# Chunk 0's channel tiles added into one, the softmax expansions kept in spent rows of x, and a new written order

## The chip, the cores and the metric

The kernel runs on one core of a Trainium2 chip. Its five engines work side by side, each through its own list of instructions in order: TensorE (PE: matrix products; its weight loads are listed apart as PEld), VectorE (DVE: elementwise work), ScalarE (ACT: activations and casts), GpSimd (POOL, which here mostly issues DMAs) and SyncE (SP, which only issues DMAs). An engine stops where an instruction has to wait for a semaphore of another engine or of a DMA, and all that is queued behind it stops too. The metric is the device time of one execution in microseconds, the median of several runs.

## The reference

The input x has 2048 rows of 640 bf16 numbers. It is normalised by row; one branch is local attention, the other a two-layer network, and both are added to x.

```python
xn = _layernorm(x, axis=-1)
return x + _A_ref(xn, A_wqkv, A_wo) + _B_ref(xn, B_w1, B_b1, B_w2, B_b2)
```

Attention has 32 heads of 20 channels. Each position looks at 8 positions: itself and those 2, 4, ... 14 rows before; positions before the first are masked.

```python
logits = jnp.einsum("bhsd,bhswd->bhsw", q, kg) * scale
attn = _softmax(logits, axis=-1)
o = jnp.einsum("bhsw,bhswd->bhsd", attn, vg)
```

The network is gelu(xn @ w1 + b1) @ w2 + b2 with 1536 hidden units.

## The kernel before

The 2048 rows are cut into four chunks (n = 0 to 3) of 512, a chunk into four blocks (j, or bl) of 128 rows. Channels lie on the partitions in five tiles of 128, in an order that puts four channels of each of the 32 heads into each tile. The work is cut into 659 small pieces; a string, ORDER (lines 42 to 74), lists their names, and the pieces are issued in exactly that order. Each engine so gets its part of ORDER as its own list. The names, with n the chunk:

- *Norm.* su, ng, sq: sums and squares of a block on ACT (chunks 2 and 3); st: statistics on DVE (chunks 0 and 1); rs: square root on ACT (loads an activation table); rc: reciprocal on DVE; xn: the normalised block on ACT for n > 0 (L266, pool lnp); tc: its transposition, a DMA from SP (L295).
- *Projections.* pj{n}{which}{tile} on PE (L339; which = 0, 1, 2 for q, k, v), five matmuls of 512 columns into a PSUM buffer of pool psA, which has six; pc casts the buffer to SBUF on ACT (L403) and so frees it. hj and hc are the same for halves of chunk 0 (L383, L398). pad copies the 14 columns before a chunk.
- *Logits.* qk{n}{j}{h} on DVE (L436): products of q with four shifted windows of k, all five channel tiles, into half[j, h]. pa{n}{j}{k} on DVE (L471) adds channel tiles: k = 0 adds tiles 2 and 3 onto 0 and 1 (four times 512 columns), k = 1 adds tile 1 onto 0, k = 2 tile 4 onto 0. lg{n} on PE (L479) sums the remaining tiles over channels with the 0/1 matrix head_of, one accumulation step for each tile that is left. KEPT[n] says how many pa steps are made: 2 means k = 0 and 1, and tiles 0 and 4 are left; 1 means all three, and only tile 0 is left.
- *Softmax.* cl casts the logits (ACT, L492), mask (chunk 0 alone), m and mx maximum and its subtraction (DVE, L502 to L508), ex the exponential (ACT, L519, loads a table), ss, ri, at: sum, reciprocal, product (DVE).
- *Values.* xd{n}{j} is a DMA from SP (L554) that spreads a block's weights over each head's channels. Its target, ax_view (L544), is a buffer of its own (pool axp) for chunks 0 and 2, and rows 0 to 6 of x_sb, the loaded x, for chunks 1 and 3. av{n}{j}{h} on DVE (L563) multiplies v's windows by it, again into half. aa adds the two halves: for chunks 0 to 2 as an accumulating DMA issued by POOL (L573), for chunk 3 on DVE (L575). ab and ot (L582, L586) add the rest on DVE; ot writes oT.
- *Network and output.* f1{n}_{ft} on PE (L595), into psA; ge on ACT (L611), which frees that buffer and writes hT (pool hp, 18 buffers; chunk 3 uses spent projection weights). o{n}{bl}{pc} on PE (L631, L633): pc = 0 to 3 multiply hT by w2, pc = 4 multiplies oT by wo. oc casts the sum into osb (ACT, L638), od adds it to the output in DRAM (a DMA from POOL, L644).
- *Output's start.* xp{n} writes rows of x to the output (SP, L304): xp0 rows 0 to 3 of the 16 row blocks, xp1 rows 4 to 7, xp2 rows 8 to 14. xb{n} adds the bias b2 there (POOL, L308). xl adds b2 to the last block on DVE (L311), which oclo and ochi add to the last output.

On DVE the chunks run in pairs: logits of 0, logits of 1, values of 0, values of 1, then the same for 2 and 3, because both use half. The loops are only in the names; what stands when is ORDER's.

Of the kernel before, what the change touches and what calls it, by code (L numbers as in the profile page):

```python
# [23 lines left out]
BPC = CH // P  # L24
# [21 lines left out]
st13a st13 hj112 hc112 st10 st12 rs1 qk010 rc1 qk000 qk011 hj110 f10_0 ge0_0 hj212 xn13 qk001 xn10 tc13 xn11 hc212  # L46
pa010 hj011 hj010 hc010 f10_11 f10_2 hc110 hc011 qk031 qk021 ge0_11 f10_10 qk020 pa000 su23 f10_6 xn12 ge0_10 qk030
pa020 su21 tc10 tc11 su22 hj200 hc200 f10_3 ge0_3 pa030 pa011 f10_9 tc12 xp0 su20 ng2 sq21 ge0_9 pa021 pj101 pc101
ge0_2 sq23 pj111 pj102 pj114 pc114 xp2 pc102 pj110 pc110 pj104 pa001 ge0_6 pa031 lg0 pc111 cl0 ldo xb3 xb2 pc104 mask
m0 mx0 ex0 pj112 pj103 pc103 pj113 pc113 ss0 ri0 pad11 pj100 pc100 pc112 qk121 qk120 hj211 sq20 hc211 qk101 ld2 pj124  # L50
qk100 sq22 pc124 f10_4 rs2 f11_6 pj121 rc2 ge0_4 pa120 qk110 f11_2 f10_1 ge0_1 pa121 qk111 xn21 pj123 pc123 ge1_6
pa122 pa100 pa110 xn23 f10_7 ge0_7 f11_8 tc23 f11_0 o000 xn20 tc20 tc21 ge1_2 f10_5 ge1_0 xb0 xn22 tc22 qk131 at0 xd00
ge1_8 f11_3 ge1_3 pa111 qk130 su32 pa101 pc121 f10_8 ge0_8 pad02 hj210 f11_5 pa130 pj120 pc120 pj200 pc200 pa112 pj211
pc211 pj210 pj212 pa131 pa102 pc210 hc210 pad12 pa132 lg1 av000 cl1 pj202 ge0_5 pj214 pc202 pj204 av001 aa00 m1 xd02
av021 pad21 av020 xd01 av011 av010 pj220 pj203 su33 ge1_5 su31 su30 ng3 sq33 xd03 av031 o001 pc212 pc203 o002 pc214
sq30 ab00 ot00 aa02 aa01 sq32 sq31 pj213 pc213 xp1 pj221 pj224 rs3 av030 ab02 pj122 pc122 pad22 rc3 ot02 o003 o004
oc00 od00 pj201 mx1 ex1 ss1 ri1 at1 xn31 pc220 xn30 f11_9 o020 o021 o022 o023 xd10 ab01 ot01 pc204 o024 oc02 pc201
aa03 tc30 ab03 f11_4 pc224 o030 o031 o032 pj223 o033 ot03 o034 xn33 av100 f12_3 av101 aa10 xn32 pc223 xd12 av120 xd13
f12_0 f11_11 av130 oc03 pc221 o010 o011 ge2_3 f12_11 o012 ge2_11 ge1_4 ge1_9 xd11 av110 av111 aa11 o013 o014 av121
pj222 pc222 av131 aa13 tc31 tc33 tc32 pj302 pj322 pj300 pc322 pj314 pc314 pj312 ab10 f11_1 ge1_11 ge1_1 f11_7 pj303  # L60
qk201 ot10 qk200 pa200 pc312 ge2_0 pj301 pc301 ab11 pa201 f11_10 pc302 ge1_10 qk211 ot11 od02 qk210 ab13 qk231 ot13
pj324 pc324 pj304 pc304 pa210 qk230 aa12 qk221 ab12 ge1_7 pj311 pa211 oc01 ot12 pa230 od01 f13_2 qk220 pc311 f12_8
pa212 od03 ge3_2 pa220 pc300 o130 pa231 pj313 pa221 o131 o132 o133 o134 oc13 pj310 f13_0 pc303 pc310 ge2_8 xb1 o120
pa202 pa232 pa222 lg2 o121 o122 pad31 pc313 qk300 f13_6 qk311 cl2 m2 qk310 f13_10 qk331 mx2 ge3_6 f13_8 qk330 ge3_0
f13_3 ge3_3 pa310 o123 qk301 o124 ex2 ss2 oc12 od12 f12_7 qk320 ri2 pa311 at2 xd23 pa330 pa300 qk321 f12_4 o110 o111
o112 pa301 o113 ge3_10 f12_10 pa320 pa312 o114 oc11 ge2_10 f12_6 f13_7 ge3_7 ge3_8 ge2_7 o100 o101 pa321 f12_2 xd21
od13 pa331 pa302 pa322 f12_5 o102 o103 ge2_6 ge2_5 o104 pa332 lg3 od11 oc10 od10 pj323 av210 pc323 av211 f12_9 cl3 m3
f13_1 xd22 xd20 ge3_1 pj321 av230 f12_1 ge2_1 aa21 av231 f13_5 ge3_5 av201 av200 aa23 f13_9 mx3 ge2_2 ge2_4 aa20 ab21
f13_4 ge2_9 ot21 ex3 ss3 ri3 ge3_4 f13_11 ge3_11 av220 ab23 o210 o211 at3 xd30 o212 o213 o214 ot23 oc21 od21 av221
aa22 pj320 o330 ab20 pc321 ot20 ge3_9 pad32 pc320 av300 o310 av301 o200 o201 o202 o203 o204 oc20 od20 o311 o230 o231  # L70
xd31 av310 o232 xd32 o233 o234 oc23 o312 o220 o221 o222 av311 aa31 ab22 ot22 o223 o224 od23 oc22 od22 av321 o313 av320
aa32 ab32 ot32 o320 o321 o322 o323 o324 oc32 od32 ab31 ot31 o314 oc31 od31 o300 xd33 o301 o302 o303 aa30 av331 ab30
ot30 o304 oc30 od30 av330 aa33 ab33 ot33 o331 o332 o333 o334 ohi xl oclo ochi ochd
""".split()


# [1 line left out]
def kernel(  # L78
# [101 lines left out]
    mask = consts.tile([H, W, MW], BF16, name="mask")  # L180
# [292 lines left out]
    def do_lg(n):  # L473
        tiles["L", n] = [psA.tile([P, W // 2, P], F32, tag="acc", name=f"L{h}") for h in range(2)]
        ts = {KT: range(KT), 3: (0, 1, 4), 2: (0, 4), 1: (0,)}[KEPT[n]]
        for h in range(2):
# [65 lines left out]
        )  # L542

    def ax_view(n):  # L544
        if n % 2 == 0:
            return get(("ax", n), lambda: axp.tile([P, BPC, W, P], BF16, tag="ax", name="ax"))[:]
        return (
            x_sb[:, 0 : 2 * BPC, :]
            .rearrange("p b d -> p (b d)")[:, 0 : BPC * W * P]
            .rearrange("p (j w c) -> p j w c", j=BPC, w=W)  # L550
        )

    def do_xd(n, j):
        nc.sync.dma_start(  # L554
            ax_view(n)[:, j, :, :],
            tiles["attn", n][j * H : (j + 1) * H, :, :].unsqueeze(1).to_broadcast([H, NQ, W, P]),
        )


    def do_av(n, j, h):  # L560
        cs = slice(j * P, (j + 1) * P)
        ws = slice(W // 2 * h, W // 2 * (h + 1))
        nc.vector.tensor_tensor(  # L563
            out=half[:, j, h],
            in0=window(qkv_tile(n, 2), h, cs),
            in1=ax_view(n)[:, j, ws, :].unsqueeze(2).to_broadcast([P, W // 2, KT, P]),
            op=ALU.mult,
        )
# [140 lines left out]
    for n in range(NCH):  # L709
# [87 lines left out]
```

## Time and profile before

| | |
|---|---|
| median of 3 runs | 205.94 us (205.85 to 206.23) |
| the profiled execution | 205.63 us |
| its span, first to last instruction | 203.9 us |
| granted TensorE clock | 0.999 of full speed |
| moved by DMA | 31.77 MB |

The span is what the profile's times count from; some 1.7 us of the execution lie outside it. A row of a group reads: line, engine, operation, output and input, shape and count, then busy us and mean ns of one, then the idle time of the engine before it. A row of the timeline reads: start, time to the end of the last of its instructions, engine, line, operation, count, and in brackets the idle time before it and who ended it. Matmuls overlap, so in the chain of waits a run of them is counted by the time by which it advances.

### The profile page before, as it was taken

The page shows a single profiled execution, that of the slowest core. Times are in us where ns is not written, and L with a number is a line of the kernel's source. Part 1 is how long each engine was busy: PE and PEld are TensorE (multiplying, and loading weights), DVE is VectorE, ACT ScalarE, POOL GpSimd, SP SyncE. Part 2 cuts the span into 40 slices and gives each one's busy share as a digit, 9 for nine tenths or more (in the row PEclk, how much of TensorE's full clock was granted, in tenths as well). Part 3 has the DMA queues.
Part 4 walks back from the last instruction along what each step waited for, and adds up shares of the span by engine and source line. Part 5 has one row for each costly group of instructions (what it writes and reads, how often), then busy time and mean ns, then how long its engine had stood idle before and what let it go on. Part 6 is the DMA issues. An engine that isn't in the chain of part 4 may idle for free.

```text
span 203.9 us, 3209 instructions
## 1 busy us (share of the span) xinstructions
PE 199.0 (98%) x1239; PEld 111.7 (55%) x1261; DVE 181.5 (89%) x226; ACT 127.1 (62%) x246; POOL 34.6 (17%) x49
## 2 busy tenths in 40 slices
PE   8999999999999999999999999999999999999994
PEld 3998565564464555554555554445544455555552
DVE  2699999499998997879999998999999999799991
ACT  5589999999967998856335825473625793111210
POOL 2000000440000243002350060003104224111120
PEclk9999999999999999999999999999999999999999
DMA  6999469899358399999999076005552997972154
GB/s 212 392 395 380 109 217 327 300 259 200 84 112 269 74 172 166 162 146 189 186 178 180 0 88 109 0 0 69 107 130 34 174 190 120 206 110 30 27 66 64
DMA packets 27335, 31.77 MB, mean 156 GB/s; under 512 B 9272, under 2 KB 22072, under 8 KB 27320
## 3 DMA queue, kind: packets, MB, share of 16 engines
q0 software_dynamic: 7408, 12.78, 39.2%
q1 hardware_dynamic: 19600, 18.58, 31.7%
q8 instruction: 10, 0.16, 0.3%
q10 hardware_dynamic: 312, 0.20, 0.3%
q14 instruction: 5, 0.04, 0.1%
HBM read 10.00 MB, written 7.54 MB: 86 GB/s over the span
## 4 chain that ended last, share of the span: by engine, by line
PE 98%; issue 1%; DVE 0%
PE lo L631 28%; PE hps L595 25%; PE pps L339 24%; PE hi L633 8%; PE gps L383 7%; PE idle L449 2%; PE gps L352 1%; PE L L479 1%; PE tp L283 0%; DVE xnT L288 0%; DVE osb L661 0%; PE tb L459 0%
## 5 line engine op out<-in xcount | busy, mean ns | idle before, releaser
L595 PE MATMUL hps<-xnT,w_sb 128*128 128x512 bf16 x234 | 55.2, 379 | 0.3
L436 DVE TENSOR_TENSOR half<-qT,kT 128x2560 bf16<-128x2560 bf16 x32 | 46.6, 1483 | 1.1 <-PE L L479 1.0
L631 PE MATMUL lo<-w_sb,hT 128*128 128x512 bf16 x137 | 40.1, 379 | 0.0
L595 PEld LDWEIGHTS <-w_sb 128*128 128x128 bf16 x240 | 23.1, 98 | 26.2
L471 DVE TENSOR_TENSOR half<-half 128x1024 bf16<-128x1024 bf16 (+1 forms) x44 | 36.5, 878 | 0.0
L633 PE MATMUL hi<-w_sb,hT 128*128 128x128 bf16 x144 | 31.5, 219 | 0.4
L638 ACT CAST osb<-lo 128x512 bf16<-128x512 f32 x15 | 8.8, 583 | 37.1 <-PE hi L633 18.3
L611 ACT ACTIVATE hT<-hps,b1T 128x512 bf16<-128x512 f32 x36 | 24.0, 692 | 6.5 <-PE hps L595 5.6
L644 POOL DMA_DIRECT2D out_dram<-osb x15 | 13.7, 958 | 72.3 <-ACT osb L639 72.3
L563 DVE TENSOR_TENSOR half<-vT,x_sb 128x2560 bf16<-128x2560 bf16 x16 | 23.0, 1486 | 2.8 <-DMA x_sb<-e 2.6
L573 POOL DMA_DIRECT2D half<-half x12 | 15.6, 1302 | 54.9 <-DVE half L563 54.9
L563 DVE TENSOR_TENSOR half<-vT,ax 128x2560 bf16<-128x2560 bf16 x16 | 23.0, 1482 | 1.2 <-PE L L479 1.2
L631 PEld LDWEIGHTS <-hT 128*128 128x128 bf16 x144 | 14.1, 98 | 17.2 <-issue 0.4
L631 PE MATMUL lo<-wo,oT 128*128 128x512 bf16 x75 | 22.3, 379 | 0.1
L339 PE MATMUL pps<-xnT,wq_sb 128*128 128x512 bf16 x74 | 18.5, 379 | 0.1
L339 PE MATMUL pps<-xnT,wv_sb 128*128 128x512 bf16 x73 | 18.2, 379 | 0.1
L339 PE MATMUL pps<-xnT,wk_sb 128*128 128x512 bf16 x74 | 18.0, 379 | 0.1
L633 PE MATMUL hi<-wo,oT 128*128 128x128 bf16 x80 | 16.9, 219 | 0.2
L176 ACT ACT_TABLE_LOAD x12 | 15.4, 1283 | 0.9 <-PEq L781 0.7
L633 PEld LDWEIGHTS <-hT 128*128 128x128 bf16 x144 | 14.1, 98 | 1.9
L582 DVE TENSOR_TENSOR half<-half 128x1280 bf16<-128x1280 bf16 x16 | 13.1, 820 | 0.4 <-DMA half<-half 0.3
L403 ACT CAST vT<-pps 128x512 bf16<-128x512 f32 x15 | 8.8, 586 | 6.9 <-PE pps L339 6.9
(91 smaller groups left out, 263.4 us busy)
## 6 DMA issues: line engine op xcount, KB each, us to landing
half<-half POOLq DMA_DIRECT2D x12, 640.0 KB, 6.8
w_sb<-in_B_w_dram SPq DMA_DIRECT2D x4, 960.0 KB, 11.8
out_dram<-osb POOLq DMA_DIRECT2D x15, 160.0 KB, 3.7
ax<-e SPq DMA_DIRECT2D x8, 256.0 KB, 4.8
x_sb<-e SPq DMA_DIRECT2D x8, 256.0 KB, 4.9
out_dram<-b2bc POOLq DMA_DIRECT2D x3, 640.0 KB, 9.6
x_sb<-in_A_x_dram SPq DMA_DIRECT2D x1, 1280.0 KB, 13.9
out_dram<-x_sb SPq DMA_DIRECT2D x2, 640.0 KB, 4.7
```

Source lines behind the costliest of these rows:

```text
L176: nc.scalar.activation(warm[:], nc.const_aps.tensor(0.0, [P, 1], F32), func)
L339: nc.tensor.matmul(ps[:], lhsT=wqkv_p[which][:, ti, to, :], rhs=xnT[:, ti, :], start=(ti == 0), stop=(ti == KT - 1),)
L383: nc.tensor.matmul(ps[:, to - a, :], lhsT=wqkv_p[which][:, ti, to, :], rhs=tiles["xnT", 0][:, ti, pair * 2 * P : (pair + 1) * 2 * P], star ...
L436: nc.vector.tensor_tensor(out=half[:, j, h], in0=q[:, :, at].unsqueeze(1).to_broadcast([P, W // 2, KT, P]), in1=window(k, h, at), op=ALU.mult,
L471: nc.vector.tensor_tensor(out=kept, in0=kept, in1=gone, op=ALU.add)
L563: nc.vector.tensor_tensor(out=half[:, j, h], in0=window(qkv_tile(n, 2), h, cs), in1=ax_view(n)[:, j, ws, :].unsqueeze(2).to_broadcast([P, ...
L573: nc.gpsimd.dma_start(a, b, accum_op=ALU.add, max_dma_last_dim=CUT)
L595: nc.tensor.matmul(ps[:], lhsT=w1_sb[:, ti, ft * P : (ft + 1) * P], rhs=tiles["xnT", n][:, ti, :], start=(ti == 0), stop=(ti == KT - 1),)
L611: nc.scalar.activation(hT, tiles["hps", n, ft][:], ACT.Gelu_apprx_tanh, bias=b1T[:, ft : ft + 1], scale=1.0)
L631: nc.tensor.matmul(lo[:], lhsT=lhs, rhs=rhs[:, 0:CH], start=first, stop=last)
L633: nc.tensor.matmul(hi[:, 0 : D - CH], lhsT=lhs, rhs=rhs[:, CH:D], start=first, stop=last)
L644: nc.gpsimd.dma_start(rows, tiles["osb", n, bl][:], accum_op=ALU.add)
```

## The change

KEPT[0] goes from 2 to 1, so that four pieces are new, pa002, pa012, pa022 and pa032, and lg0 has one accumulation step instead of two. Chunks 0 and 2 lose their own expansion buffer and use rows 0 to 6 of x_sb; chunks 1 and 3 use rows 8 to 14. The pools of xn, hT and osb have 4, 24 and 3 buffers instead of 3, 18 and 2. ORDER is new behind the first seventy-odd pieces. Line numbers of the new file are lower by 1 from its line 115 on and by 2 behind ax_view.

```diff
-KEPT = (2, 1, 1, 1)
+KEPT = (1, 1, 1, 1)
...
-    lnp = ctx.enter_context(tc.tile_pool(name="lnp", bufs=3))
+    lnp = ctx.enter_context(tc.tile_pool(name="lnp", bufs=4))
...
-    axp = ctx.enter_context(tc.tile_pool(name="axp", bufs=1))
...
-    hp = ctx.enter_context(tc.tile_pool(name="hp", bufs=18))
-    outp = ctx.enter_context(tc.tile_pool(name="outp", bufs=2))
+    hp = ctx.enter_context(tc.tile_pool(name="hp", bufs=24))
+    outp = ctx.enter_context(tc.tile_pool(name="outp", bufs=3))
...
     def ax_view(n):
-        if n % 2 == 0:
-            return get(("ax", n), lambda: axp.tile([P, BPC, W, P], BF16, tag="ax", name="ax"))[:]
+        first = n % 2 * 2 * BPC
         return (
-            x_sb[:, 0 : 2 * BPC, :]
+            x_sb[:, first : first + 2 * BPC, :]
```

ORDER of before, from where the two part to lg1's surroundings:

```
st13a st13 hj112 hc112 st10 st12 rs1 qk010 rc1 qk000 qk011 hj110 f10_0 ge0_0 hj212 xn13 qk001 xn10 tc13 xn11 hc212
pa010 hj011 hj010 hc010 f10_11 f10_2 hc110 hc011 qk031 qk021 ge0_11 f10_10 qk020 pa000 su23 f10_6 xn12 ge0_10 qk030
pa020 su21 tc10 tc11 su22 hj200 hc200 f10_3 ge0_3 pa030 pa011 f10_9 tc12 xp0 su20 ng2 sq21 ge0_9 pa021 pj101 pc101
ge0_2 sq23 pj111 pj102 pj114 pc114 xp2 pc102 pj110 pc110 pj104 pa001 ge0_6 pa031 lg0 pc111 cl0 ldo xb3 xb2 pc104 mask
m0 mx0 ex0 pj112 pj103 pc103 pj113 pc113 ss0 ri0 pad11 pj100 pc100 pc112 qk121 qk120 hj211 sq20 hc211 qk101 ld2 pj124
...
pc211 pj210 pj212 pa131 pa102 pc210 hc210 pad12 pa132 lg1 av000 cl1 pj202 ge0_5 pj214 pc202 pj204 av001 aa00 m1 xd02
```

ORDER of after, from where the two part to behind chunk 1's products with v, and its last stretch:

```
st13a pad02 st13 hj110 hc110 st10 st12 rs1 f10_1 ge0_1 qk001 rc1 qk010 xn11 tc11 qk011 xn10 tc10 qk000 pa010 pa000
f10_2 hj112 xn13 hc112 pa011 xn12 tc12 hj011 hc011 f10_0 ge0_0 hj010 hc010 qk021 hj211 su23 qk030 f10_11 f10_9 ge0_9
hc211 f10_8 ge0_8 qk031 pa012 tc13 qk020 xp0 ldo xb0 pad11 f10_6 pa030 pa020 ge0_2 su22 pj111 ge0_6 pc111 pj103 su20
pj114 su21 ng2 sq23 pa001 ge0_11 pj113 pc113 pa031 pa021 pa002 pj110 f11_11 sq22 pc103 f11_1 xp2 ge1_1 ge1_11 pc110
pa022 f11_5 ge1_5 f10_7 ge0_7 pa032 lg0 cl0 mask pc114 m0 pj104 mx0 ex0 ss0 pj100 pc100 pj112 pc104 pj101 pc101 pj102
pc112 pc102 pj124 f10_4 ri0 qk131 qk110 qk101 f11_0 sq20 sq21 rs2 rc2 ge1_0 xn20 qk121 ld2 o000 qk130 qk111 f11_4
ge1_4 pj123 f10_10 ge0_10 f11_6 ge1_6 xn22 tc20 ge0_4 hj210 xn23 hc210 at0 f11_10 hj212 f10_3 hj200 xn21 hc212 pad12
tc22 qk100 tc23 f10_5 hc200 ge0_5 ge0_3 pa110 pa130 pa100 pa111 pj120 pc120 su32 qk120 pj121 pc121 pa112 tc21 pj200
f12_7 pa120 pj211 pa131 pc124 ge2_7 xd00 xp1 su33 pc211 pa101 pc200 pj213 pa121 pa102 pc123 pj204 pc204 su30 su31
pa132 o001 pa122 lg1 xd03 f12_2 ng3 av000 av001 cl1 xd02 f12_8 ge2_8 ge1_10 ge2_2 aa00 pj122 f12_5 pc213 av020 av021
aa02 pc122 sq32 ge2_5 av030 av031 aa03 pj223 sq30 pj203 m1 mx1 pj202 pc202 ab00 ot00 xd01 av010 pc203 pj210 ex1 pad21
sq31 sq33 rs3 av011 aa01 o002 o003 f11_3 pj214 pc210 pc214 o004 oc00 rc3 xn30 pj220 ss1 ri1 at1 pc220 xn33 xl xd11
pj224 pc224 xd10 pj212 tc33 xd12 ab03 ot03 f11_2 ab02 ot02 ab01 ot01 av111 av101 xn31 xn32 av110 aa11 av120 f12_6 o020
o021 o022 o023 pc212 o024 oc02 f11_8 av121 pad22 o030 tc32 o031 xd13 av100 pc223 o032 o033 o034 oc03 f12_11 ge2_11
o010 o011 o012 aa12 av131 ge1_2 pj201 pc201 ge1_8 tc30 tc31 o013 o014 f13_10 av130 aa13 pj311 pj313 pc311 pc313 ab11
...
o224 o331 av320 av321 aa32 ab32 ot32 o313 oc22 od22 od20 o320 o321 o322 o323 o324 oc32 od32 ot31 o314 o300 o301 o302 o303
av301 oc31 od31 av331 aa30 ab30 ot30 o304 aa33 oc30 od30 ab33 ot33 o332 o333 o334 oclo ohi ochi ochd
```

More of the change, by code (lines that the diff above doesn't have):

```diff
@@ L45 @@
 hc100 xn03 tp03 tc03 pk hj202 rc02 xn02 tp02 tc02 gc4 hj201 hc201 hj111 st11a st10a hc111 st12a hj012 hc012 st11 hc202
[L46 to L73, printed above, removed]
+st13a pad02 st13 hj110 hc110 st10 st12 rs1 f10_1 ge0_1 qk001 rc1 qk010 xn11 tc11 qk011 xn10 tc10 qk000 pa010 pa000
@@ new lines @@
+sq31 sq33 rs3 av011 aa01 o002 o003 f11_3 pj214 pc210 pc214 o004 oc00 rc3 xn30 pj220 ss1 ri1 at1 pc220 xn33 xl xd11
+pj224 pc224 xd10 pj212 tc33 xd12 ab03 ot03 f11_2 ab02 ot02 ab01 ot01 av111 av101 xn31 xn32 av110 aa11 av120 f12_6 o020
+o021 o022 o023 pc212 o024 oc02 f11_8 av121 pad22 o030 tc32 o031 xd13 av100 pc223 o032 o033 o034 oc03 f12_11 ge2_11
+o010 o011 o012 aa12 av131 ge1_2 pj201 pc201 ge1_8 tc30 tc31 o013 o014 f13_10 av130 aa13 pj311 pj313 pc311 pc313 ab11
+pj310 qk211 pj302 pc302 ot11 qk210 qk221 pa210 ab12 f12_4 pa211 ge2_4 qk231 pj303 ge1_3 ab13 ot12 pc303 aa10 ot13 od02
@@ new lines @@
+f12_3 pc310 f11_9 pj324 pc324 f12_0 ge2_0 qk220 qk201 pj312 ab10 od00 ge1_9 pc312 pj300 pc300 pa220 ot10 qk230 qk200
+pa212 pj314 pc314 pa230 xb2 oc01 pj304 pc304 od01 pj301 pc301 pa221 pa200 f13_9 ge3_9 f12_9 pa231 f11_7 ge3_10 pa201
+o130 o131 ge1_7 o132 o133 pa222 pa202 xb3 pad31 pa232 lg2 qk310 qk301 qk311 cl2 m2 qk331 f12_1 o134 oc13 qk300 mx2
+qk320 pj322 pc322 pj321 pj221 pc321 ge2_9 pj222 pc222 ge2_6 xb1 qk321 qk330 ge2_1 o120 od13 pa300 pa330 ex2 ss2 o121
+o122 o123 pa301 ri2 pa302 f13_4 ge3_4 at2 xd21 o124 oc12 od12 f13_8 ge3_8 xd22 f13_7 ge3_7 pc221 pad32 o110 o111 xd20
@@ new lines @@
+o112 o113 o114 oc11 f13_0 pa310 xd23 pa320 o100 od11 o101 o102 ge3_0 o103 o104 oc10 od10 pa311 pa321 pa312 pa322 pa331
+pa332 lg3 av210 f13_2 av211 ge3_2 f13_6 ge3_6 av201 f13_5 ge3_5 cl3 ge2_3 av200 od03 av231 f13_3 ge3_3 m3 mx3 f13_11
+ge3_11 f13_1 pj320 pc320 f12_10 ge2_10 ex3 o210 o211 o212 o213 av230 aa21 ab21 ot21 o214 oc21 pj323 ss3 ri3 at3 aa20
+ab20 o200 o201 ot20 o202 o203 o204 av220 xd33 ge3_1 o330 av221 aa23 ab23 ot23 aa22 pc323 av330 o310 xd30 av300 oc20
+o230 o231 o232 o233 o234 oc23 od23 xd31 av311 o311 o312 av310 aa31 ab31 od21 xd32 o220 o221 o222 o223 ab22 ot22 o224
@@ L74 @@
+o331 av320 av321 aa32 ab32 ot32 o313 oc22 od22 od20 o320 o321 o322 o323 o324 oc32 od32 ot31 o314 o300 o301 o302 o303
+av301 oc31 od31 av331 aa30 ab30 ot30 o304 aa33 oc30 od30 ab33 ot33 o332 o333 o334 oclo ohi ochi ochd
 """.split()
```

## The prediction

> **What bounds the kernel now.** The page comes first: the engines' busy time and the chain that ended last (span 203.9 us).
>
> ```profile
> PE 199.0 (98%) x1239; PEld 111.7 (55%) x1261; DVE 181.5 (89%) x226; ACT 127.1 (62%) x246; POOL 34.6 (17%) x49
> ...
> PE 98%; issue 1%; DVE 0%
> ```
>
> TensorE (PE) is busy in 98% of the span and carries the whole chain. Busy need not mean that it never waited, so the waits of PE come next, and a stretch of the chain in order of time (start, length, what).
>
> ```profile
> PE idle L449 <- PEq L781: 0.8, 1, 0.8
> PE gps L352 <- DVE xnT L288: 0.2, 1, 0.2
> ```
>
> ```profile
> 29.05 6.47 PE pps L339 x30
> 35.52 0.98 PE L L479 x16
> 36.50 0.34 PE pps L339
> 36.85 0.05 issue
> ```
>
> After the first 6.2 us PE waits for nobody: 30 projection matmuls take 6.47 us, 0.216 each, and the holes are 0.05 us. So the time is the sum of PE's work plus the start and the tail. It can fall by what PE is spared and by the few holes left, and it rises by every new wait of PE. The other engines matter where PE reaches a piece that needs them.
>
> **What goes: eight matmuls.** With KEPT[0] = 1 the logits of chunk 0 (lg0, L479) are summed over one tile instead of two, 8 matmuls instead of 16. The row above has 16 in 0.98 us; chunk 1 already has 8:
>
> ```profile
> 64.45 0.55 PE L L479 x8
> ```
>
> 0.98 - 0.55 = **0.43 us** less on PE. No other piece of PE changes its work; they only change places.
>
> **What is added: four DVE additions**, pa002 to pa032, of the form that the other chunks have:
>
> ```profile
> L471 DVE TENSOR_TENSOR half<-half 128x1024 bf16<-128x1024 bf16 x28 | 17.9, 683 | 0.0
> ```
>
> ```profile
> 121.66 4.83 DVE L471 TENSOR_TENSOR half<-half 128x1024 bf16<-128x1024 bf16 x7
> ```
>
> One lasts 683 ns, but the next starts before it ends: of the seven in 4.83 one has double size (1.13), so 1.13 + 5 x 0.60 + 0.70. I take 4 x 0.60 = 2.4 us more on DVE ahead of lg0. That is no time of the kernel until PE has to wait for it, so I put both engines' due times side by side.
>
> ```profile
> 30.41 4.76 DVE L471 TENSOR_TENSOR half<-half 128x2048 bf16<-128x2048 bf16 x6
> 37.23 0.21 DVE L496 TENSOR_TENSOR Lb<-Lb,mask 32x128 bf16<-32x128 bf16 x1 [2.06 <-ACT Lb L492]
> ...
> 42.78 5.63 DVE L436 TENSOR_TENSOR half<-qT,kT 128x2560 bf16<-128x2560 bf16 x4
> ...
> 60.03 4.23 DVE L471 TENSOR_TENSOR half<-half 128x1024 bf16<-128x1024 bf16 x6
> 64.97 2.89 DVE L563 TENSOR_TENSOR half<-vT,ax 128x2560 bf16<-128x2560 bf16 x2 [0.71 <-PE L L479]
> ```
>
> *At lg0.* DVE ends chunk 0's additions at 35.17 now, so at about 37.6. The new order puts more before lg0 on PE: 16 pieces of five 512-column matmuls (5 x 0.216 = 1.08) where there were 13, one small group less (0.55): +2.7 us. PE comes at 35.52 + 2.7 = 38.2. No wait.
>
> *At lg1.* From lg0 the chain mask, maximum, exponential, sum, reciprocal is the same; ACT reaches cl0 behind the casts and Gelus that the order puts ahead, 0.3 us later than it could. So chunk 1's products begin at 42.78 + 2.7 = 45.5. From there to the end of its additions the same instructions run in another order: 64.26 - 42.78 = 21.5, end at 67.0. PE has 2.55 us more work before lg1 than now: 64.45 + 2.55 = 67.0. A tie, as it was before.
>
> ```profile
> 127.00 0.62 PE L479 MATMUL L<-half,head_of 128*32 128x512 bf16 x8
> ```
>
> *At lg2* the order puts PE only 0.64 us later than now (at lg3 too): 127.64. So DVE must win back some 2 us between lg1 and lg2. In the run before it idles there for 0.71 (row above), 1.48 and 1.19:
>
> ```profile
> 81.96 0.69 DVE L525 TENSOR_TENSOR sums<-e 128x512 f32<-128x512 bf16 x1 [1.48 <-ACT e L519]
> ...
> 89.29 11.70 DVE L563 TENSOR_TENSOR half<-vT,x_sb 128x2560 bf16<-128x2560 bf16 x8 [1.19 <-DMA x_sb<-e]
> ```
>
> The 1.48 goes: mx1 now stands behind m1, and four pieces (ab00, ot00, av010, av011; 4.0 us) lie over the exponential. In its place come about 0.75 for rc3 behind ACT's rs3 (two squares and a table load after ex1) and 0.4 for xl, which must wait for xn33. The wait for xd1 shrinks to some 0.2. By these sums chunk 1's products with v start near 90.6 (now 89.29), and 11.70 + 25.5 later (100.99 to 121.66 + 4.83 = 126.49 now) DVE is ready for lg2 at 127.8, against 127.64 plus what PE has lost by then: 0.2 of wait. From lg2 to lg3 both sides keep their distance.
>
> ```profile
> 174.37 5.70 DVE L563 TENSOR_TENSOR half<-vT,x_sb 128x2560 bf16<-128x2560 bf16 x4 [1.42 <-DMA x_sb<-e]
> ...
> 197.79 0.49 DVE L586 TENSOR_TENSOR oT<-half 128x640 bf16<-128x640 bf16 x1
> ```
>
> ```profile
> 198.87 1.24 PE L631 MATMUL lo<-wo,oT 128*128 128x512 bf16 x4
> ```
>
> *At the end.* DVE's last sum stands at 198.28 now and PE asks for it at 198.9. After lg3 DVE has the same instructions in both orders; lg3 comes some 0.85 later, the exponential of chunk 3 about 0.3 nearer to its reader, and the 1.42 for xd3 goes, as xd33 leaves 5 us ahead of its reader. So DVE ends near 198.0, and PE, with 0.43 less before it and 0.2 lost, asks at 198.7. No wait.
>
> **The casts between.** Two orders with equal sums differ in how long a PSUM buffer stays taken; there are six in psA, and PE waits when the ACT piece that frees one is late. Chunk 0 and 1's casts, Gelus and norms fill ACT:
>
> ```profile
> 40.00:60.00 20.00, 19.89 (x105) 10.79 (x106) 19.47 (x21) 18.46 (x34) 2.83 (x4) 1.00 0.84 173
> ```
>
> ```profile
> 53.48 1.28 ACT L611 ACTIVATE hT<-hps,b1T 128x512 bf16<-128x512 f32 x2
> 54.70 0.92 ACT L266 ACTIVATE xn<-x_sb,nmr,rstd 128x640 bf16<-128x640 bf16 x1
> ```
>
> ```profile
> 56.72 1.25 PE L383 MATMUL gps<-xnT,wv_sb 128*128 128x256 bf16 x10
> ```
>
> (Columns of the first: window, length, busy PE, PEld, DVE, ACT, POOL.) ACT has 18.46 of 20 us. In the old order a buffer is free some 2 us before PE asks: ge1_0, the second Gelu of the row at 53.48, ends at 54.76, and hj210 takes its buffer at 56.72. In the new one pc124, pc123 and ge1_10 come 10 us and more after their matmuls, so three or four buffers are left to turn, and ACT runs some 2 us later than now (2.7 with chunk 0's sums, 0.6 less because hc211 and pad11 stand earlier). By the steps between neighbours on ACT (a Gelu 0.58, a norm 0.81, a cast 0.48: their lengths less some 0.11 of overlap) ge1_4 ends at 52.5 where hj210 asks at 52.4, hc210 at 56.35 where hj200 asks at 56.3, hc212 at 57.45 where f10_5 asks at 57.4. Not shown in the run before, so bounded: at best nothing, and no gain, as PE doesn't wait now; at worst each of the three by ACT's own slip since 40 us, about 0.4, which is 1.2. I take **0.25**, near the lower end, as each lands within 0.1 of its due time.
>
> **The buffers.** hT 24, xn 4, osb 3: each can only take a wait off ACT, and PE waits for none of them now, so nothing; below nothing only through the order that they permit. The expansions: xd0 and xd2 go to rows 0 to 6 of x, xd1 and xd3 to rows 8 to 14 (same size, same queue). New are two waits. xd03 and those behind it stand on SP behind xp1, which reads rows 4 to 7:
>
> ```profile
> 52.24 5.22 SPq L295 DMA_TRANSPOSE xnT<-xn x4
> 58.14 3.38 SPq L554 DMA_DIRECT2D ax<-e x4
> ```
>
> ```profile
> ax<-e SPq DMA_DIRECT2D x4, 256.0 KB, 4.1
> out_dram<-x_sb SPq DMA_DIRECT2D x1, 640.0 KB, 6.1
> ```
>
> (The last: size and us to landing, of 52 to 75 us.) Behind the four transposes, some 1 us later than now (58.4), and xd00 (0.85) xp1 goes out at 59.3 and lands within 6.1 (a time that it took beside four expansions), so xd03 goes by 65.4, xd02 one issue later, landing 4.1 on, by 70.4. Its reader av020 is due at 70.4 on DVE. Nothing else waits on SP there. So nothing to a few tenths on DVE; I take nothing. And xd1 and xl must follow the norms of chunk 3, counted above. xb2 and xb3 (bias into the output) go from 38 us to places between 105 and 125 on POOL, before od pieces that nothing reads until the osb turn comes round, several us later: nothing.
>
> **Sum.** -0.43 + 0.25 at the casts; the 0.2 at lg2 is the same delay met again, not another. That is -0.18 on the profiled execution: span 203.7, time 205.63 - 0.18 = 205.45. The median of the runs is 205.94, 0.31 above the profiled one, so the forecast is **205.76 us**. A measurement here can tell about 0.2% (0.41 us) from no change; the forecast is within it.
>
> **Rivals.**
> - *The cover is complete* (chance 0.30). All dues above are ties, and ties may fall PE's way; the weight loads of three lg wait for DVE now, 1.1 in all, of which about 0.1 each reaches PE, and a DVE with more slack would give it back.
>
> ```profile
> PEld L479 <- DVE half L471: 1.1, 3, 0.4
> ```
>
> For: the order before is as tight and costs nothing. Then 205.94 - 0.43 = 205.5, with the lg holes 205.2.
> - *A DVE late at lg2* (0.32, the slower side). The place is the accumulating transfers of half, of which ab11 is due first after chunk 1's products, at 90.6 + 11.7 = 102.3, with aa11 issued after the third product, 94.9: 7.4 us.
>
> ```profile
> DMA to landing us min/median/max: 5.6/6.8/9.7
> ```
>
> Up to 7.4 it is hidden; from there each us goes to lg2 and so to the end, for DVE has no gap in the 25.5 us between, and PE none either. At 9.7 that is 2.3: 208.1; at 8.4, 1.0 and 206.8. The casts at their upper bound of 1.2 give the same sign, 206.7. Against it is the wait that such a piece shows now:
>
> ```profile
> DVE half L582 <- DMA half<-half: 0.3, 1, 0.3
> ```
>
> - *POOL held by DVE* (0.03, inside the one above). The issue of these transfers takes 1.2 us while DVE multiplies without a gap:
>
> ```profile
> 156.19 1.21 POOL L573 DMA_DIRECT2D half<-half x1 [1.67 <-DVE half L563]
> ```
>
> If such an issue had to wait for the end of the running product (1.49), aa11 would land 1.5 later and lg2 lose 0.9: 206.7. The Trainium skill, page "SBUF — State Buffer", section "SBUF: two separate sides", says that a DMA issued from GpSimd needs a port that some VectorE instructions lock for their whole length, so its descriptors wait. By that rule a DVE with less idle time would delay these transfers. The row speaks against it.
> - *The change does not act as written*: no; on PE and DVE the two kernels' instructions differ by these eight matmuls and four additions alone.
>
> **Chances.** Forecast with small PE waits (0 to 0.6, so 205.5 to 206.1) 0.38; complete cover, 205.1 to 205.5, 0.30; late DVE or casts, 206.1 to 208.1, 0.32. A tenth of the first (0.04) lies under 205.53, and as much of the third under 206.35. Faster by over 0.2% 0.34, within 0.2% 0.38, slower 0.28. The range 205.1 to 206.9 leaves out about 0.13 on the slow side and less on the fast.
>
> **What would show it.** L479 with x8 at lg0 in 0.55 us; four more L471 of 683 ns; lg0 near 38.2, lg1 67.1, lg2 127.9, lg3 153.4; in the waits of PE or its weight loads, rows for hps, gps or pps on ACT between 50 and 60 with some 0.25 together. A wait of PE for DVE at L479 over 0.5, a DVE wait at L563 on x_sb<-e near 70, or at L582 on half<-half near 102 over 0.5, would prove the slower rival; no PE wait at all, the faster.

## The result and the profile after

The changed kernel takes **208.08 us** (median, 207.70 to 208.98) against 206.03 us (205.85 to 206.23) of the kernel before: ratio 1.0101, 95% interval 1.0071 to 1.0132. It is 1% slower; forecast were 205.76 us, within 205.1 to 206.9. The profiled execution took 207.70 us, its span is 205.8 us. Medians here and below are of all executions, while the ratios leave out those over 1.5% above the fastest of their kernel (without them the medians of "changed, once more", "aa11 sooner, 16 more" and "aa11 later" below are 208.08, 208.94 and 208.36).

The page of the kernel after, busy time of the engines and shares of the chain that ended last:

```profile
PE 199.7 (97%) x1231; PEld 111.8 (54%) x1253; DVE 184.1 (89%) x230; ACT 127.3 (62%) x246; POOL 34.4 (17%) x49
...
PE 62%; DVE 20%; DMA 10%; issue 5%; SPq 1%; ACT 0%; POOLq 0%; DVEq 0%
```

The chain was PE's for 98% before. Now over a third of it lies elsewhere, 20% on DVE and 10% on DMA. The chain in order of time says where (start, length, what):

```profile
38.64 0.55 PE L L478 x8
...
95.61 8.43 DMA half<-half
104.13 0.83 DVE half L580
...
122.99 6.49 DVE half L470 x9
129.52 0.59 PE L L478 x5
```

The chain leaves PE at chunk 2's logits (lg2, 129.52), goes back through DVE's additions to the sum ab11 (L580, 104.13), and from there to one accumulating transfer, aa11, that was issued at 95.61 and landed 8.43 us later. The waits of the kernel after, first of PE, then of DVE (in total, times, longest):

```profile
PE hps L593 <- DMA xnT<-xn: 0.3, 1, 0.3
...
PE L L478 <- DVE half L470: 0.2, 1, 0.2
```

```profile
DVE Lb L495 <- ACT Lb L491: 2.4, 1, 2.4
...
DVE half L580 <- DMA half<-half: 1.8, 1, 1.8
```

PE's two rows are new: 0.3 us for chunk 3's transposed tiles, 0.2 us at the logits. DVE's wait for a transfer of half was 0.3 and is 1.8 us. Places in both profiles, with the forecast between (us):

| | before | forecast | after |
|---|---|---|---|
| third x tile's transposes on PE | 12.04 | 12.04 | 12.46 |
| lg0 | 35.52 | 38.2 | 38.64 |
| lg1 (by the timeline, where the chain's 64.45 is 64.38) | 64.38 | 67.0 | 67.43 |
| first product of chunk 1 | 89.29 | 90.6 | 91.03 |
| chunk 1's first accumulating transfer: issue, to landing | 92.48, 7.1 | 94.9, up to 7.4 | 95.61, 8.4 |
| first sum behind chunk 1's products | 100.91 | 102.3 | 104.13 |
| lg2 | 127.00 | 127.9 | 128.92 |
| last output group | 198.87 | 198.7 | 200.38 |
| span | 203.9 | 203.7 | 205.8 |

The rest of the sum: PE's eight matmuls of lg1 last 0.80 us (unhindered 0.62, the row of lg2 before), and lg2 is cut in two:

```profile
128.92 0.40 PE L478 MATMUL L<-half,head_of 128*32 128x512 bf16 x3
129.52 0.59 PE L478 MATMUL L<-half,head_of 128*32 128x512 bf16 x5 [0.21 <-DVE half L470]
```

Before, PE began lg2 0.15 us behind the start of the matmul ahead of it and needed 0.55; now the last matmul ahead starts at 128.60 and the piece behind lg2 at 130.05: 1.45 in place of 0.70, a loss of 0.75. So against the 203.47 us (203.9 - 0.43) that PE's work alone would give: 0.42 at the start, 0.2 at lg1, 0.3 at the transposed tiles, 0.75 at lg2, 0.4 behind PE's last matmul (its end to the end of the span: 3.23 us, was 2.84), and about 0.25 that stays unexplained: 205.8.

### The profile page after: what moved, and what is told of

Read it like the earlier page. It is cut to its first block, busy times and chain, and to the rows that moved or that the text cites. A ratio compares the mean times of both kernels' runs of the same rounds, so it can differ in the third digit from the quotient of the medians.

```text
span 205.8 us, 3190 instructions
## 1 busy us (share of the span) xinstructions
PE 199.7 (97%) x1231; PEld 111.8 (54%) x1253; DVE 184.1 (89%) x230; ACT 127.3 (62%) x246; POOL 34.4 (17%) x49
## 4 chain that ended last, share of the span: by engine, by line
PE 62%; DVE 20%; DMA 10%; issue 5%; SPq 1%; ACT 0%; POOLq 0%; DVEq 0%
PE lo L629 20%; PE hps L593 17%; PE pps L338 13%; DMA half<-half 7%; PE hi L631 6%; PE gps L382 5%; DVE half L561 5%; DVE half L435 5%; DVE half L470 5%; DMA x_sb<-in_A_x_dram 3%; DVE half L580 2%; DVE oT L584 1%; DVE stats L211 1%; PE L L478 1%; PE tp L282 0%
## 5 line engine op out<-in xcount | busy, mean ns | idle before, releaser
L593 PE MATMUL hps<-xnT,w_sb 128*128 128x512 bf16 x233 | 56.0, 379 | 0.7 <-DMA xnT<-xn 0.3
L561 DVE TENSOR_TENSOR half<-vT,x_sb 128x2560 bf16<-128x2560 bf16 x32 | 45.6, 1485 | 1.5 <-PE L L478 1.1
L435 DVE TENSOR_TENSOR half<-qT,kT 128x2560 bf16<-128x2560 bf16 x32 | 46.2, 1484 | 0.0
L470 DVE TENSOR_TENSOR half<-half 128x1024 bf16<-128x1024 bf16 (+1 forms) x48 | 38.5, 859 | 0.0
L609 ACT ACTIVATE hT<-hps,b1T 128x512 bf16<-128x512 f32 x36 | 23.5, 686 | 5.1 <-PE hps L593 5.1
L571 POOL DMA_DIRECT2D half<-half x12 | 14.3, 1235 | 72.5 <-DVE half L561 72.5
L629 PE MATMUL lo<-wo,oT 128*128 128x512 bf16 x78 | 22.8, 379 | 0.0
L338 PE MATMUL pps<-xnT,wq_sb 128*128 128x512 bf16 x75 | 18.0, 380 | 0.1
L338 PE MATMUL pps<-xnT,wv_sb 128*128 128x512 bf16 x71 | 17.6, 379 | 0.2
L580 DVE TENSOR_TENSOR half<-half 128x1280 bf16<-128x1280 bf16 x16 | 13.0, 820 | 1.9 <-DMA half<-half 1.8
L629 PEld LDWEIGHTS <-oT 128*128 128x128 bf16 x80 | 7.8, 98 | 9.6 <-DVE oT L584 0.6
L307 POOL DMA_DIRECT2D out_dram<-b2bc x4 | 7.4, 2080 | 33.1 <-DMA b2bc<-in_B_b_dram 33.1
```

Of the source, the lines that this page charges most:

```text
L338: nc.tensor.matmul(ps[:], lhsT=wqkv_p[which][:, ti, to, :], rhs=xnT[:, ti, :], start=(ti == 0), stop=(ti == KT - 1),)
L435: nc.vector.tensor_tensor(out=half[:, j, h], in0=q[:, :, at].unsqueeze(1).to_broadcast([P, W // 2, KT, P]), in1=window(k, h, at), op=ALU.mult,
L470: nc.vector.tensor_tensor(out=kept, in0=kept, in1=gone, op=ALU.add)
L561: nc.vector.tensor_tensor(out=half[:, j, h], in0=window(qkv_tile(n, 2), h, cs), in1=ax_view(n)[:, j, ws, :].unsqueeze(2).to_broadcast([P, ...
L571: nc.gpsimd.dma_start(a, b, accum_op=ALU.add, max_dma_last_dim=CUT)
L580: nc.vector.tensor_tensor(out=a, in0=a, in1=b, op=ALU.add)
```

## The experiments

Times are medians; the ratio is to the kernel before on the same chip, with its 95% interval. "Fetch" is the quarter microsecond in which, between 90 and 100 us, a packet of the queue q8 (instruction) moves; "landing" and "wait" are those of aa11 and of DVE for it. These columns are of the one profiled execution of each kernel. The kernels were timed in sets on several chips, so across sets the ratios compare better than the times.

| kernel | us | ratio | fetch | issue, landing | wait |
|---|---|---|---|---|---|
| changed, once more | 208.56 | 1.0102 (1.0059 to 1.0146) | 97.50 | 95.4, 8.2 | 1.6 |
| aa11 sooner | 219.36 | 1.0627 (1.0577 to 1.0676) | 97.25 | 94.0, 14.9 | 6.9 |
| reader ab11 later | 208.69 | 1.0132 (1.0081 to 1.0184) | 97.75 | 95.6, 9.0 | 2.4 |
| two tiles again | 206.48 | 1.0013 (0.9995 to 1.0032) | 95.00 | 95.6, 6.7 | 0 |
| 16 instructions more | 206.32 | 1.0006 (0.9976 to 1.0037) | 94.50 | 95.4, 7.2 | 0.6 |
| aa11 sooner, 16 more | 209.55 | 1.0146 (1.0102 to 1.0191) | 94.75 | 94.2, 14.5 | 6.5 |
| 60 more | 206.66 | 1.0028 (1.0006 to 1.0050) | 95.25 | 96.0, 6.8 | 0.2 |
| old order, one tile | 210.10 | 1.0181 (1.0141 to 1.0221) | 98.75 | | |
| aa11 later | 208.52 | 1.0104 (1.0077 to 1.0130) | 98.00 | 98.7, 6.1 | 0.9 |
| plain copies | 206.95 | 1.0046 (1.0023 to 1.0068) | 97.50 | 95.7, 7.4 | 0.7 |
| 8 more | 208.79 | 1.0119 (1.0086 to 1.0152) | 97.00 | 95.4, 7.7 | 1.1 |
| before, 16 more | 206.26 | 1.0016 (0.9999 to 1.0034) | 93.50 | | |
| aa11 sooner, plain copies | 206.62 | 1.0039 (1.0009 to 1.0069) | 97.75 | 94.1, 8.3 | 0.3 |
| plain copies, 16 more | 206.47 | 1.0022 (0.9995 to 1.0048) | 95.25 | 96.0, 6.7 | 0 |

### First set: the place of aa11, and the added work

Four kernels on one chip. The first is the changed kernel, unaltered:

> The changed kernel once more, unaltered, as the base for the three beside it. First theory (the queue): DVE waits about 1.8 us for the first accumulating transfer of chunk 1 again and lg2 loses about 0.7 us of PE again, time 207.7 to 208.5 us. The 0.4 us by which the x tile of the second transposes came late at the start (12.46 against 12.04 us) and the 0.35 us longer tail are either chance, then some of it is gone here, or they belong to this kernel, then both are here again.

Measured 208.56 us, with the wait of 1.6 us again. The third x tile's transposes start at 12.27 here, and in the other kernels anywhere between 12.08 and 12.88: that delay goes with the run.

```
-... ot01 av111 av101 xn31 xn32 av110 aa11 av120 f12_6 ...
+... ot01 av111 xn31 xn32 av110 aa11 av101 av120 f12_6 ...
```

> The changed kernel, with the product av101 moved behind aa11, so that the first accumulating transfer of chunk 1 is issued after two products as before, not after three. First theory (the place of aa11 costs the wait): the issue comes 1.4 us sooner, at about 94.2 us, it lands by 102.6, the wait of 1.81 us at L580 falls to 0 to 0.4, lg2 starts 0.6 to 0.7 us sooner, and the time falls by 0.6 to 0.9 us against the unaltered kernel beside it (to some 207.3). Rival (the queue is full as a whole): the wait moves to the next transfer or the transfer takes 1.4 us longer, and the time stays within 0.3 us of the unaltered kernel.

Both theories fell: 219.36 us, 11 us more. The transfer was issued 1.4 us sooner and landed at 108.9, 5 us later than in the changed kernel. PE's longest wait:

```profile
PE hps L593 <- DMA xnT<-xn: 10.8, 1, 10.8
```

Part of the loss is the clock: when PE went on, the granted clock was 0.50 (114 to 118 us), then 0.74, and 1.00 only from 120 us on.

So the first theory, that the place behind a third product alone costs the wait, was wrong. Something else holds this transfer up, and it holds up the transposes of chunk 3 too.

```
-ab11 pj310 qk211 pj302 pc302 ot11 qk210 qk221
+pj310 qk211 pj302 pc302 qk210 ab11 ot11 qk221
```

> The changed kernel, with the reader ab11 moved behind two of chunk 2's key products (2.8 us of DVE work that needs no transfer), aa11 left where it is. First theory: the wait is covered, lg2 starts 0.6 to 0.7 us sooner, time 0.6 to 0.9 us less than the unaltered kernel. Rival (the queue is full as a whole): the same here, as the reader can wait; only where the wait does not matter for lg2 at all (DVE late for another reason) does the time stay within 0.3 us.

208.69 us: no gain. The try was ill chosen: qk211 and qk210 write where aa11 reads and where ab11 reads, so they wait for the same landing (DVE, L435 on half<-half: 2.4 us), and ab11 sums other products than it should. It tells nothing of the theories; it shows only that these two products hang on aa11 as well.

```
-KEPT = (1, 1, 1, 1)
+KEPT = (2, 1, 1, 1)
 (pa002, pa012, pa022, pa032 taken from ORDER)
```

> The changed kernel with chunk 0 again summed down to two tiles: the four additions pa002 to pa032 are left out and lg0 has 16 matmuls; order and buffers stay new. First theory (the additions lie in the time in which DVE waits for lg0 anyway, and the loss is elsewhere): 0.43 us more on PE and nothing won, time 0.3 to 0.6 us above the unaltered kernel. Rival (the 2.4 us of added DVE work is what makes DVE late at lg1 and lg2): the waits at lg1 and lg2 go and the time falls by 0.3 to 0.9 us.

206.48 us, 2.1 us below the changed kernel, as the rival said, but not for its reason. DVE's wait for lg0's cast grows by just the additions that went:

```profile
DVE Lb L495 <- ACT Lb L491: 4.9, 1, 4.9
```

4.9 against 2.4: the additions lie in DVE's idle time, as forecast. And aa11 is issued at 95.58 here, at 95.61 in the changed kernel; it lands after 6.7 us, not 8.4. Same instructions around it, same time of issue, another landing. What differed had to be in the transfers.

### What the transfers do

The transfers of the kernel after from 98 to 100 us, GB/s in steps of 0.05 us, then queues (packets, MB, packet time as a share of 16 DMA engines; q0 has the accumulating transfers, q1 those of SP, transposes among them):

```profile
GB/s 287 727 102 36 87 538 108 0 0 51 51 0 0 0 0 0 0 5 10 5 10 10 5 10 10 10 10 5 15 5 10 56 0 102 0 512 0 308 0 512
...
q0 software_dynamic: 57, 0.15, 142.4%
q1 hardware_dynamic: 152, 0.03, 28.6%
```

For some 1.2 us next to nothing moves: two steps of 51, otherwise 0 to 15 GB/s. A step at 5 GB/s is one packet of 256 B, the last of a transpose. The 57 packets of q0 meanwhile take 142% of the engines' time, 0.80 us each on average: they have begun and don't get on. The same stretch with two tiles:

```profile
GB/s 548 154 31 282 425 154 0 307 410 102 0 358 359 102 0 410 307 102 0 512 205 102 0 615 154 51 51 563 205 0 51 563 205 0 102 563 154 0 102 512
...
q0 software_dynamic: 167, 0.43, 112.3%
q1 hardware_dynamic: 67, 0.01, 4.1%
```

No hole; aa11 moves at full pace from 98.0, 0.22 us for a packet of q0. Of 96 to 98 us in the kernel after:

```profile
q1 hardware_dynamic: 609, 0.31, 97.2%
q8 instruction: 1, 0.02, 3.5%
```

Amid the transpose a packet of 16 KB moves on the instruction queue; 3.5% of 16 engines in 2 us is one DMA engine for 1.1 us, about the length of the hole. With two tiles that packet falls between 94 and 96, ahead of the last two transposes (the 16 instructions of PE in lg0's other half move the later blocks of its program). The new theory: **a block of instructions falls into a transpose, which ends a microsecond later, and an accumulating transfer hardly moves until a transpose that stands before it has ended.**

### Second set: only the fetch is moved

```
-        do_warm(WARM, CH)
+        do_warm(WARM - 8, CH)
+        do_warm(16, CH // 2)
```

Eight of ten idle matmuls at the start become sixteen of half the width; no other instruction changes.

> The changed kernel, only that 8 of the 10 idle matmuls of 512 columns at the start are cut into two of 256 columns (same columns, 8 matmuls and 8 weight loads more, as many instructions as the kernel with two tiles had more). Theory (the block of instructions): the trace shows a fetch on the instruction queue q8 at 97.5 us, amid chunk 3's last two transposes, in every kernel whose transfers then stall (10 GB/s for 1 us and more), and at 95.0 in the kernel with two tiles, which doesn't stall; with 16 instructions more the fetch falls near 95.0, the transfers land in about 7 us, DVE doesn't wait at L580, and the time falls by 1.5 to 2.5 us, to 205.9 to 206.4. Rival 1 (the added DVE work makes DVE late): no change, 207.7 to 208.6. Rival 2 (the transposes and the accumulating transfers collide whatever the fetch does): no change, and the hole at 98.5 us stays.

206.32 us: 2 us gone (ratio 1.0006, where the changed kernel has 1.0101 and 1.0102). The fetch is at 94.5; all issues stand where they did in the changed kernel's second profile (aa11 95.43 in both, the last two transposes from 94.31, there 94.37). DVE still waits 0.6 us for aa11, which lands after 7.2. From 98 to 100 us:

```profile
GB/s 169 579 102 0 154 564 102 0 154 563 102 0 307 410 102 0 410 307 102 0 410 307 102 0 461 256 102 0 614 102 108 51 512 154 56 102 512 154 51 159
```

With four times ten of 128 columns (60 instructions more):

> The changed kernel with all 10 idle matmuls cut into four of 128 columns: 30 matmuls and 30 weight loads more, so the fetch comes 60 instructions sooner, some 4 to 6 us, near 92 us, ahead of the last two transposes and amid the first two. Theory (the block of instructions): no stall at 98.5; a smaller one near 92 may come, which no accumulating transfer meets; time 205.9 to 206.6. Rivals: no change, 207.7 to 208.6.

206.66 us, no hole at 98.5. The fetch came at 95.25, not near 92, among the last packets of the transpose issued at 91.86: this one landed after 5.8 us, where the one in its place took 4.2 to 4.3 in the other kernels of the new order, and no accumulating transfer stood behind it. The place was forecast badly, the effect rightly. With four idle matmuls cut (8 more):

> The changed kernel with 4 of the 10 idle matmuls cut in two, 8 instructions more. Theory (the block of instructions): if the fetch stays at or above 96.5 the hole and 207.7 to 208.6 us stay; if it comes at 95.5 or sooner, no hole and 206.0 to 206.6. A time that does not go with the place of the fetch speaks against the theory.

The fetch came at 97.0, above the bound of 96.5, and the loss stayed: 208.79 us. Here it reaches PE by the transposes themselves: the last of them lands after 9.1 us, and PE waits 1.5 us for xnT. The control, 16 more in the kernel before:

> The kernel before with 8 idle matmuls cut in two, as a control: the cut itself costs PE and the start nothing, and its transfers have 8.4 us until their reader comes. Theory: 205.8 to 206.3, no difference, wherever the fetch falls. If the cut itself gains or loses time at the start, it shows here as over 0.4 us.

206.26 us, and the fetch hardly moved (93.50, before 93.25). The cut is free within the uncertainty; what a fetch elsewhere would do to this kernel it doesn't show.

### Third set: transposes and accumulating transfers

The kernel with aa11 sooner, and eight idle matmuls cut:

> The kernel with aa11 issued after two products (219.4 us), with the same 8 idle matmuls cut in two. Theory (the block of instructions): the fetch moves from 97.25 to about 95.0, the collapse from 98.5 to 104 us goes, and with it 13 us: 205.6 to 206.4. Rival (aa11 issued just ahead of the last transposes collides with them by itself): still above 215.

Half right. Four of six executions took 208.9 to 210.2, two 219.2 and 220.4, as all six did without the cut. The profiled one is the last and collapsed though the fetch stood at 94.75. So with aa11 issued ahead of the last two transposes the collapse needs no fetch in them; what decides among executions stays open, and so does why the other four are still above 206.4.

```
-... xn32 av110 aa11 av120 f12_6 ...
+... xn32 av120 av110 aa11 f12_6 ...
```

> The changed kernel with the product av120 moved ahead of av110, so that aa11 is issued 1.4 us later, at about 97.0 us, and its first packets come after the last two transposes have moved theirs (they ended at 98.1 us where nothing stalled). Theory (transposes and accumulating transfers hold each other up where their packets meet, and the block of instructions at 97.5 only keeps the transposes long enough to meet): no hole, the last transposes land in under 6.5 us, not 8.1, PE doesn't wait for xnT, aa11 lands at about 103.7, no later than when it was issued 1.4 us sooner (104.0), and the time falls by 0.3 to 0.8 us against 208.1 to 208.6. Rival (the block of instructions alone slows the transposes): they still land in 7.9 us or more, aa11 lands near 105.4, time 208.8 to 209.5.

Half right again: the last transposes landed in 5.7 and 4.0 us, PE didn't wait for xnT, aa11 landed in 6.1, at 104.8; but the time did not fall, and the hole did not go. As av120 now came before its expansion, DVE waited 1.2 us on x_sb<-e and 0.9 on aa11, and the total was the same, 208.52. The hole stands at 98.9 to 100.0, with the fetch at 98.0 and before any packet of aa11 has moved: the late end is the transpose's own; what the accumulating transfer adds is that it waits.

```
     def do_td(n, bl):
...
+        if n == 3 and bl < 2:
+            xn = tiles["xn", n, bl][:].rearrange("p (t m) -> p t m", t=KT)
+            nc.sync.dma_start(xnT[:, :, bl * P : (bl + 1) * P], xn)
+            return
         nc.sync.dma_start_transpose(xnT[:, :, bl * P : (bl + 1) * P], tiles["xn", n, bl][:])
```

> The changed kernel, in which the last two transposes of chunk 3 (tiles 0 and 1) are plain copies of the same bytes to the same place, in packets of 256 B as well; the transposition of these two tiles is left out, all waits stay. The block of instructions comes at 97.5 as in the changed kernel. Theory (the transposes must be there for the stall): no hole at 98.5, aa11 lands in about 7 us, no wait of PE on xnT, time 205.8 to 206.5. Rival (small packets or a full queue do it): hole and time as in the changed kernel, 207.7 to 208.6.

206.95 us, fetch at 97.5 as in the changed kernel. From 98 to 100 us both queues move side by side:

```profile
GB/s 246 179 200 282 241 108 230 189 379 10 266 118 287 174 174 174 282 230 133 220 143 225 174 282 72 338 220 174 159 133 271 215 220 61 384 215 123 159 184 323
...
q0 software_dynamic: 138, 0.35, 92.4%
q1 hardware_dynamic: 227, 0.06, 19.0%
```

The copy of 256 B packets shares the engines with the accumulating transfer; the transpose did not. The copies also go out sooner (SP issues both in 2.1 us, the transposes in 4.3), so more than the transposition differs. The last two kernels close the square (their place in it and the kernel that they start from stand in the expectations):

> The changed kernel with the last two transposes as plain copies (transposition left out) and 8 idle matmuls cut in two: the fourth case beside transposes with the fetch at 97.5 (208.1 to 208.6), transposes with the fetch at 94.5 (206.32) and copies with the fetch at 97.5 (206.95). Theory (the fetch costs time only as it prolongs a transpose for which the accumulating transfer waits): no difference to the copies with the fetch at 97.5, 206.5 to 207.1. Rival (the fetch costs by itself): 1.5 us or more below them, 205.0 to 205.5.

206.47 us. With copies, moving the fetch is worth 0.5 us by the medians, and the intervals overlap; with transposes it was 2. The copies themselves land sooner too with the fetch moved (4.0 and 7.0 us, not 5.1 and 8.1).

> The kernel with aa11 issued after two products (219.4 us), in which the last two transposes of chunk 3 are plain copies of the same bytes; the transposition of these two tiles is left out. Theory (an accumulating transfer that is under way when a transpose comes holds both up): without transposes no collapse, aa11 issued at 94.0 lands by 102, DVE doesn't wait, PE doesn't wait for xnT: 206.2 to 207.0. Rival (four transfers at once are too many for the queues, of whatever kind): collapse as before, above 212.

206.62 us where transposes gave 219.36. The collapse was theirs; four transfers at once are not too many. From 98 to 100 us in the collapsed kernel:

```profile
GB/s 82 92 189 184 681 51 154 67 123 56 56 51 0 0 0 5 0 0 0 0 0 51 0 0 0 5 0 51 0 0 0 5 0 51 0 0 0 5 51 0
...
q0 software_dynamic: 24, 0.06, 141.6%
q1 hardware_dynamic: 154, 0.04, 26.6%
```

The Trainium skill, page "DMA: Bandwidth & Descriptors", section "Rules for kernel authors", says: "A transpose next to ordinary DMAs needs nothing". The sentence is about transposes that spoil each other's data and says nothing of time. In time the runs here differ beside an accumulating transfer: 12.7 us between the kernel with transposes and the one with copies, the halved clock after PE's wait included.

### The bare change

```
-KEPT = (2, 1, 1, 1)
+KEPT = (1, 1, 1, 1)
 (old order; pa002, pa012, pa022, pa032 each right behind pa001, pa011, pa021, pa031)
```

> The kernel before with the one change of KEPT: chunk 0 summed down to one tile, each of the four additions set right behind the additions that it needs, the old order and the old buffers otherwise. By the prediction's sums: DVE ends chunk 0's additions at 37.6, PE comes to lg0 at 35.5 and waits 2.1 us; less the 0.43 us of lg0 that is 1.5 to 2.2 us more than before, 207.5 to 208.4, with a wait of PE on L471 of about 2 us. If the additions were hidden without the new order, the time would be 205.5 to 205.9.

210.10 us, 1.7 us above the top of the forecast. The wait is as expected, 2.2 us in two holes:

```profile
36.97 0.40 PE L479 MATMUL L<-half,head_of 128*32 128x512 bf16 x3 [1.27 <-DVE half L471]
38.29 0.59 PE L479 MATMUL L<-half,head_of 128*32 128x512 bf16 x5 [0.93 <-DVE half L471]
```

What follows was not (window, length, busy PE, PEld, DVE, ACT, POOL, granted clock):

```profile
36.00:38.00 2.00, 0.40 (x3) 0.10 (x4) 1.93 (x4) 0.30 (x1) 0.00 (x0) 1.00 0.93 184
38.00:40.00 2.00, 1.61 (x8) 0.67 (x9) 0.43 (x2) 1.30 (x3) 1.53 (x2) 0.82 1.02 374
40.00:42.00 2.00, 1.88 (x5) 0.76 (x5) 1.66 (x5) 1.86 (x4) 2.00 (x3) 0.50 1.07 396
42.00:44.00 2.00, 2.00 (x10) 0.87 (x8) 0.99 (x2) 1.51 (x3) 0.70 (x2) 0.83 1.16 246
```

```profile
40.54 2.31 PE L339 MATMUL pps<-xnT,wq_sb 128*128 128x512 bf16 x5
```

After the two holes the granted clock falls to 0.50, and five matmuls that take 1.08 us start to start elsewhere take 2.14 (40.54 to the next piece at 42.68). What the clock lacks of full speed, (1 - 0.82) + (1 - 0.50) + (1 - 0.83) = 0.85, times 2 us, is a loss of 1.7 us. The profiled execution (211.05 us, span 209.3) is 5.4 us longer than that of the kernel before: -0.43 + 2.2 + 1.7 is 3.5 of it, and 1.3 lie behind PE's last matmul (4.2 us to the end of the span, was 2.84); 0.6 stays unexplained. Some new order is needed: in the old one the additions stand in PE's way.

## Why the prediction was wrong

- **Eight matmuls, 0.43 us: right.** lg0 takes 0.55 us for eight.
- **The additions are hidden ahead of lg0: right.** lg0 came at 38.64 for 38.2, all of it (0.42) from the start; DVE had 2.4 us left, and 4.9 without the additions.
- **lg1 a tie: right in place, short in price.** 0.2 us where nothing was set down.
- **The casts, 0.25 us: wrong.** No wait of PE on ACT is in the profile; from lg0 to lg1 PE took 28.86 us (38.57 to 67.43 by the timeline) where the forecast without the casts had 28.8 (35.45 to 64.38 is 28.93; 2.55 for 2.7 more work). The long-held buffers cost under 0.1 us.
- **The wait at lg2, 0.2 us: the step that failed.** The prediction took up to 7.4 us from aa11's issue to its reader as hidden, and left the landing at the 6.8 of the median. Both were off. The distance was 6.7 us: eight products take 11.30 us, not 11.70, and the issue came 0.3 us behind the third product. The landing was 8.4, because the transfer stood behind a transpose that a fetch of instructions had prolonged. Together 1.8 us of wait for DVE, which has no gap up to lg2; PE, itself some 1.0 us late by then (the start, lg1, and 0.3 at the transposes), lost 0.75 more. The rival "A DVE late at lg2" (0.32) named the place, the transfer, the row to look for and the sign; at 8.4 us it priced 1.0 us of wait and 206.8, measured were 1.8 us and 208.1. (At 9.7 us it had 208.1 as well: the agreement with the measured time would be luck, as the landing was 8.4 and the rest of the time came from the start, the transposes and the tail.) Its weight came from the spread of earlier landings, as if 8.4 were a bad draw. It went with what stood beside it: SP's two transposes at 94.57 and the fetch at 97.5. The prediction followed SP's queue for waits of its own and not for what it moves while POOL's transfer is on its way. The rival "POOL held by DVE" did not show: aa11's issue takes 1.19 us, chunk 1's first took 1.20 before.
- **What goes back to what.** Moving the fetch alone brings 208.1 to 208.6 down to 206.32. The rest, 206.32 against 205.5 for complete cover, is lg1 (0.2), lg2 (128.11 for 127.64, part of which is lg1 and the start), and 0.4 behind PE's last matmul (3.0 to 3.3 us to the end of the span in kernels of the new order, 3.7 in the one of 219.36; 2.7 to 2.8 in the old, 4.2 in the one of 210.10; its cause stays open). So the 0.43 us were all spent on ties, the complete cover was not reached, and no version here beats the kernel before: 206.32 is its time, at 1.0006 (0.9976 to 1.0037).

**Open.** Why a transpose and an accumulating transfer take turns rather than share, and why one that is under way when a transpose comes holds both up for 10 us, the traces don't say. The kernel before issues its first transfer amid its transposes too (92.48, between 90.74 and 95.8) and its fetch at 93.25 falls there too; it has a hole of 0.6 us (94.55 to 95.15, 5 to 15 GB/s), but lands in 7.1: why it doesn't collapse stays open. The fetch as cause rests on its place going with the loss in all kernels with transposes and aa11 where the change puts it (94.5, 95.0, 95.25: no loss; 97.0, 97.5, 97.75: loss) and on the kernels that change nothing else; the fetch could not be taken away by itself. Its place is known for one execution of each kernel. Nor does every fetch among a transpose's packets prolong it: at 94.5 and 95.0 it fell among the last packets of the transpose ahead, which landed after 4.3 us as elsewhere; at 95.25 that one took 5.8.

## What to carry to other kernels

Where a reader comes a little later than a transfer lands, don't take the landing from a median of other places: list what else is on the queues in that window, transposes first, and take the worst landing beside the like. In a program whose engines are tied to tenths of a microsecond, any change of the number of instructions ahead may also move the places where the program's own blocks are fetched; test that by adding instructions that do nothing before blaming the change. A wait of PE has two prices, its length and the clock after it.

## What the runs showed of the hardware

- One block of instructions (16 KB on q8) went with 1.4 to 2.5 us, by the medians, when it fell into the DMA transposes that an accumulating transfer stood behind (97.0 to 97.75, 208.08 to 208.79 us, against 94.5 to 95.25, 206.32 to 206.66), and with 0.5 us, within the uncertainty, beside plain copies.
- An accumulating transfer issued 0.3 us ahead of two transposes: 14.9 us to landing, 219.36 us in all; the same with plain copies: 8.3 us and 206.62.
- Two holes of PE of 1.27 and 0.93 us were followed by a granted clock of 0.82, 0.50 and 0.83 over 6 us. The Trainium skill, page "TensorE: Matmul & The Clock Gate", section "Part 1: The HAM clock gate (the "warmup" mystery)", has the clock halved after an idle window of some 3.4 us; the kernel of 219.36 us agrees (clock 1.00 until 108 us, then 0.70 and 0.50, in a wait of 10.8 us). But in these two holes PE was busy for 2.0 of the 4 us from 36 to 40 and never idle for 3.4, and the measurement decides.
